# Seven block products added up in PSUM instead of on VectorE, and the low part of x by an accumulating transfer

## Chip, cores and metric

One core of one Trainium2 chip. The metric is the device time of one execution in microseconds (us). The engines are TensorE (PE; PEld are its weight loads), VectorE (DVE), ScalarE (ACT), GpSimd (POOL) and SyncE (SP); the last three also issue transfers.

## The reference

A linear attention with a decaying state, whose output, one row per token, goes through a two-layer network with a per-channel PReLU.

```
B, H, S, D = 4, 8, 768, 48
for t in range(S):
    state = sigmoid(f_logit[t])[:, None] * state + outer(k[t], v[t])
    y[t] = q[t] @ state
x = y.transpose(0, 2, 1, 3).reshape(B * S, H * D)      # 3072 x 384
h = x @ w_in                                            # 384 x 2048
g = max(h, 0) + alpha * min(h, 0)
out = g @ w_out                                         # 2048 x 384
```

All inputs and the output are fp32.

## The kernel before, in words

The work is cut into 12 steps, 0 to 11. A step is one chunk of 128 tokens of one pair of batches (U = 2 rows of 128 tokens, so T = 256 tokens). Each step has an attention part and a network part. The network part of a step runs mostly beside the attention part of the next one.

**The order** of everything is written out by hand. `ORDER_WORDS` is a list of words; each calls one part of a step, or the next piece of a part that has several. The number ahead is the step. Each engine and each DMA queue takes its instructions in the order in which the words issue them; between engines there are only semaphores. Words that the text names: `r`, `u`, `d`, `o` and `y` are TensorE parts of the attention (raw scores, quad scores, increments, off-diagonal blocks, output `py`); `f` starts a step on ScalarE with the sigmoid; `ef`, `eq`, `ek`, `ev` are the loads of a step (issued by GpSimd from step 1 on); `X` sends the attention's output through DRAM into the token layout `xT` (in step 11 straight from `y`). Words with an `N` belong to the network:

- `Nx` (line 947, ScalarE): `xh`, the high part of x with the sign turned. `NY` (`low_of_x`, line 950): the low part, x + xh, written over `xT`. `NZ` (line 954, VectorE): the mix `xs` of both. These three exist from step 3 on.
- `Na0` to `Na7`: the first layer, eight pieces of 256 channels. From step 3 on each has two halves of six matmuls: the high weights with `xh`, then the low weights with `xT`. `Nq` scales the bank, `Nb` adds the third pass, with `xs`. Steps 0 to 2 use plain fp32.
- `Nr` (ScalarE) and `Nc` (VectorE): the PReLU, into `gate`.
- `Np`: the second layer. From step 1 on it is done by blocks: `gate` is four blocks a, A, b, B (half of the channels, row of tokens), w_out is cut into 2 x 2 blocks (b11 ... b22, with sums t1 to t4 made once), and seven products replace eight. `Nm`, `Nu`, `Nv`, `Nw` (line 1016, VectorE, in halves) are the sums of gate blocks. `product(to, of, by)` multiplies a gate block with a weight block, 16 matmuls, into the PSUM bank `to`.
- The sums of products into the output tile `o` (line 1030, VectorE; `Nk` and `Ng` at lines 1050 and 1054 are ScalarE copies), then `Ns1` and `Ns0`, the stores.

Products and pieces of the first layer share four PSUM banks (pool `psn`, `bufs=4`): a new one waits until the one four back is free.

Of the kernel before, what the change touches and what calls it, by code (L numbers as in the profile page):

```python
# [48 lines left out]
v3 2ek 1O 1O b5 0Nr7 0Nr6 0Nc6 0Nc6 b5 b5 0Np1 1H0 1H0 v4 2f 0Nc7 0Nc7 2f 1U1 1U1 0Np2 2F 2F b7 b7 2g 1U1 2F 2F 2F 1D
2F 1A0 2g 1A0 v5 2g 2g 2f 2h 2h 1H1 b6 1A0 1A1 0Np3 2p 1H1 2p 2q 0Np4 1D 2g b7 1H1 1H1 2f 1A1 2q 2G 1A1 1A1 2q b6 1y0  # L50
1y1 2G 0Np5 2G V v7 2G 1Y1 v6 0Np6 0Np7 1Y0 W1 W0 W2 2q W3 1M 1M 1M 2u0 2i 1X 1X 2i 2l 2l 2r0 2R0 2l 2l 2R0 1X 1X 1X
1X 2R0 1X 1X 1X 1X 1Na0 2R0 Y7 2t 2t 2t 2U0 2t Y4 1Na1 W7 2U0 0No0 1Na2 2k 2k 2u1 2U0 2U0 2l 2r1 3ef 2U0 2l 2k Z7 2U0
W6 Y6 3ek Y2 2U0 1Nr0 1Nc0 1Nc0 1Nr1 1Nc1 2D 2A0 2A0 2K 2K 1Na3 1Nc1 Z7 2K 2K 1Nr2 1Nc2 2A0 2A0 2R1 2R1 1Na6 Z2 1Nc2
# [107 lines left out]
def kernel(  # L161
# [779 lines left out]
    def network(n_, bp, c, x):  # L941
# [7 lines left out]
        def low_of_x():  # L949
            nc.vector.tensor_tensor(x["T"], x["T"].bitcast(F32), late["xh"].bitcast(F32), ALU.add)  # L950
# [78 lines left out]
        def plus(to, of, by, scale=UP):  # L1029
            nc.vector.scalar_tensor_tensor(to, banks[of][:, 0:DH], scale, by, ALU.mult, ALU.add)  # L1030
# [121 lines left out]
```

## Time and profile before

| | |
|---|---|
| median of three runs | 587.82 us (587.04 to 588.15) |
| profiled execution | 587.32 us, span 585.5 us |
| mean granted TensorE clock | 0.985 |
| instructions | 19400 |
| DMA | 60.53 MB, mean 103 GB/s |

The span runs from the first to the last instruction of the profiled execution; what its time has more (1.8 us) lies around it. In the rows, L and a number is the line of the kernel; a group of instructions is named by what it writes and reads; "x" and a number is its count, and the arrow after an idle time points to what ended the waiting. "PEld" work overlaps "PE" work.

### The profile page before, as it was taken

How to read it: one execution, taken by the hardware profiler on the slowest of the kernel's cores; microseconds unless marked ns; L12 is line 12 of the kernel's file. 1: busy time of each engine (PE TensorE's matmuls, PEld its weight loads, DVE VectorE, ACT ScalarE, POOL GpSimd, SP SyncE). 2: the span in 40 equal slices, each digit the busy share in tenths (PEclk: the TensorE clock that was granted, in tenths of full speed). 3: DMA queues.
4: the chain of work that ended last, by engine and by line, in shares of the span. 5: the costliest groups of instructions: out<-in, count | busy, mean ns of one | idle time of the engine just before them, and what ended most of it. 6: DMA issues, size and time to landing. Idle time of an engine off the chain costs nothing. (4 is left out here: it accounts for less than half of the span.)

```text
span 585.5 us, 19400 instructions
## 1 busy us (share of the span) xinstructions
PE 564.7 (96%) x8416; PEld 521.2 (89%) x8416; DVE 513.4 (88%) x1077; ACT 320.1 (55%) x607; POOL 50.1 (9%) x89
## 2 busy tenths in 40 slices
PE   8799999999999999999999999998999899999997
PEld 6678867788888899899899899998999899999997
DVE  7689899989989999999999989998999989976452
ACT  5779985674280574474384583465374376363330
POOL 7210000200100000000010010020010000000000
PEclk9679999999999999999999999999999999999999
DMA  8959301730532252251161262172073251231000
GB/s 294 362 163 328 128 1 43 182 83 28 120 104 82 74 138 82 76 135 57 47 191 57 66 158 55 53 192 77 28 175 90 78 130 32 68 74 30 28 1 27
DMA packets 66853, 60.53 MB, mean 103 GB/s; under 512 B 44400, under 2 KB 58352, under 8 KB 66768
## 3 DMA queue, kind: packets, MB, share of 16 engines
q1 hardware_dynamic: 59744, 37.16, 22.3%
q0 software_dynamic: 6288, 21.76, 12.6%
q8 instruction: 66, 1.08, 0.8%
q10 hardware_dynamic: 736, 0.37, 0.2%
q14 instruction: 19, 0.16, 0.1%
HBM read 44.99 MB, written 13.50 MB: 100 GB/s over the span
## 5 line engine op out<-in xcount | busy, mean ns | idle before, releaser
L990 DVE SCALAR_TENSOR_TENSOR gate<-gate,om,ph 128x256 f32<-128x256 f32 x192 | 83.7, 477 | 18.6 <-ACT gate L983 18.1
L983 ACT ACTIVATE gate<-ph 128x512 f32<-128x512 f32 x96 | 55.8, 598 | 33.3 <-PE ph L959 28.8
L973 ACT ACTIVATE ph<-ph 128x512 f32<-128x512 f32 x72 | 40.7, 580 | 49.6 <-PE ph L959 45.7
L959 PE MATMUL ph<-xh,hi 128*128 128x256 f32 x432 | 62.8, 286 | 3.2 <-DVE o L1030 1.3
L1016 DVE TENSOR_TENSOR gate<-gate 128x512 f32<-128x512 f32 x88 | 58.8, 685 | 7.1 <-PE pc L1022 4.0
L959 PE MATMUL ph<-xT,w_in_sb 128*128 128x256 f32 x288 | 64.5, 382 | 0.3 <-DVE gate L990 0.3
L1022 PE MATMUL pa<-w_out_sb,gate 128*128 128x192 f32 x352 | 61.5, 328 | 0.0
L959 PEld LDWEIGHTS ph<-xT,w_in_sb 128*128 128x128 f32 x288 | 53.9, 190 | 8.3 <-issue 0.4
L959 PEld LDWEIGHTS ph<-xh,hi 128*128 128x128 f32 x432 | 55.0, 189 | 5.9 <-issue 2.9
L959 PE MATMUL ph<-xT,lo 128*128 128x256 f32 x432 | 60.0, 280 | 0.0
L526 ACT COPY A<-q 48x512 f32<-48x512 f32 x44 | 27.2, 618 | 59.2 <-DVE q L496 58.8
L1022 PEld LDWEIGHTS pa<-w_out_sb,gate 128*128 128x128 f32 x352 | 57.2, 190 | 0.5
L959 PE MATMUL ph<-xs,sum 128*128 128x256 f32 x432 | 55.1, 278 | 1.5 <-DVE xs L954 1.5
L959 PEld LDWEIGHTS ph<-xT,lo 128*128 128x128 f32 x432 | 54.7, 188 | 0.3
L959 PEld LDWEIGHTS ph<-xs,sum 128*128 128x128 f32 x432 | 51.8, 188 | 2.1 <-ACT ph L973 1.4
L563 DVE COPY_PREDICATED scores<-inq,qu 128x224 f32<-128x224 int32 (+6 forms) x140 | 42.0, 300 | 2.8 <-PE qu L553 0.4
L544 DVE TENSOR_TENSOR scores<-scores,q 128x768 f32<-128x768 f32 (+5 forms) x60 | 37.2, 620 | 0.5
L718 DVE COPY_PREDICATED scores<-mraw,raw 128x256 f32<-128x256 int32 (+1 forms) x80 | 35.6, 445 | 1.5 <-ACT A L730 0.3
L730 ACT COPY A<-scores 32x256 f32<-32x256 f32 x80 | 32.2, 402 | 5.8 <-DVE scores L563 4.6
L410 DVE TENSOR_TENSOR qd<-qd,scores 128x768 f32<-128x768 f32 (+2 forms) x36 | 27.1, 753 | 6.0 <-ACT qd L398 6.0
L1022 PE MATMUL pe<-w_out_sb,gate 128*128 128x192 f32 x176 | 30.8, 328 | 1.0 <-DVE gate L1016 0.9
L1022 PE MATMUL pb<-t,gate 128*128 128x192 f32 x176 | 31.3, 331 | 0.0
(151 smaller groups left out, 1018.7 us busy)
## 6 DMA issues: line engine op xcount, KB each, us to landing
w_out_raw<-in_w_out SPq DMA_DIRECT2D x8, 767.8 KB, 8.7
w_in_raw<-in_w_in SPq DMA_DIRECT2D x8, 767.2 KB, 9.5
scores<-in_fT POOLq DMA_DIRECT2D x11, 512.0 KB, 4.9
q<-in_qT POOLq DMA_DIRECT2D x11, 512.0 KB, 6.2
k<-in_kT POOLq DMA_DIRECT2D x11, 512.0 KB, 7.5
turned<-q SPq DMA_DIRECT2D x40, 128.0 KB, 3.5
ksn<-turned SPq DMA_DIRECT2D x10, 512.0 KB, 3.6
out<-o SPq DMA_DIRECT2D x24, 192.0 KB, 2.0
```

The source lines that it names most:

```text
L410: nc.vector.tensor_tensor(qdv[d], qdv[d - 1][:, :, :, 1:5 - d], f[:, :, 1:5 - d].rearrange("p (g i) r -> p g i r", i=NB), ALU.mult)
L526: nc.scalar.copy(A[halves(cc)[1], :, par * HP:(par + 1) * HP, CH * cc:CH * (cc + 1)], x["q3"][rows(par)].rearrange("p (u h c) s t -> p u h ...
L544: nc.vector.tensor_tensor(to, of, spread(fq[:, :, 1:1 + n], n), ALU.mult)
L563: nc.vector.copy_predicated(ad[:, :, m:NB], inq[:, 0:n].bitcast(I32).unsqueeze(1).unsqueeze(3) .broadcast_to((128, H, n, 4)), of.rearrange ...
L718: nc.vector.copy_predicated(ad[:, :, :, d:4], diag[:, :, 0:n].bitcast(I32).unsqueeze(1).broadcast_to((128, H, NB, n)), rv[:, :, QO[d]:QO[d ...
L730: nc.scalar.copy(A[s_, u, :, s_].rearrange("p h (i t) -> p h i t", t=4), ad[s_])
L959: nc.tensor.matmul(banks[f][:, j * T:(j + 1) * T], lhsT=of[:, kt, 128 * j:128 * (j + 1)], rhs=by[:, kt], start=first_ and kt + j == 0, sto ...
L973: nc.scalar.activation(banks[f], banks[f], AF.Copy, scale=EPS - 1.0)
L983: nc.scalar.activation(to, of, AF.Relu, scale=-1.0)
L990: nc.vector.scalar_tensor_tensor(to[:, j], to[:, j], om[:, m:m + 1], of[:, j], ALU.mult, ALU.add)
L1016: nc.vector.tensor_tensor(block(to)[:, p], block(x_)[:, p], block(y_)[:, p], op)
L1022: nc.tensor.matmul(banks[to][:, 0:DH], lhsT=block(of)[:, f], rhs=of_w_out(by)[:, f], start=start and f == 0, stop=f == NH - 1, skip_group_ ...
```

## The change

Three things change.

The sums of products. Some products now add onto a bank that already holds another product (`start` is False), with a copy taken out in between where a partial sum is needed by itself. Product 1 goes to bank pc, is copied (`Nd`), product 2 is added onto it and copied again (`Ne`); product 0 goes to pa, is copied (`Nk`), product 4 is added and read (`Nh`), product 5 is added and read (`Ni`, `Nj`). Four VectorE sums (`g`, `h`, `i`, `L`) and four ScalarE copies (`d`, `k`, `e`, `j`) a step take the place of eight sums and two copies. `Nf` and `Nl` no longer exist. The signs of the sums m and u and of t4 turn so that the products can be added.

The low part of x. `NY` is now a transfer that GpSimd issues, which adds `xh` from SBUF onto `xT` in SBUF; it was a VectorE instruction.

The order. From the attention of step 1 on, the words stand in another order.

```diff
-        to, x_, y_, op = (("t3", b22, b12, ALU.subtract), ("t2", "t3", b11, ALU.add), ("t4", "t2", b21, ALU.subtract),
+        to, x_, y_, op = (("t3", b22, b12, ALU.subtract), ("t2", "t3", b11, ALU.add), ("t4", b21, "t2", ALU.subtract),
...
-            nc.vector.tensor_tensor(x["T"], x["T"].bitcast(F32), late["xh"].bitcast(F32), ALU.add)
+            nc.gpsimd.dma_start(out=x["T"].bitcast(F32), in_=late["xh"].bitcast(F32), accum_op=ALU.add)
...
-        def plus(to, of, by, scale=UP):
-            nc.vector.scalar_tensor_tensor(to, banks[of][:, 0:DH], scale, by, ALU.mult, ALU.add)
+        def copy(to, of):
+            nc.scalar.activation(to, banks[of][:, 0:DH], AF.Copy, scale=UP)
+
+        def plus(to, of):
+            nc.vector.scalar_tensor_tensor(to, banks[of][:, 0:DH], UP, to, ALU.mult, ALU.add)
...
-        for n, args in enumerate((("pa", "a", "b11"), ("pc", "A", "t3"), ("pb", "B", "t4"), ("pa", "b", "b21", False),
-                                  ("pd", "B", "t2"), ("pe", "a", "t1"), ("pf", "A", "b22"))):
+        for n, args in enumerate((("pa", "a", "b11"), ("pc", "A", "t3"), ("pc", "B", "t4", False), ("pb", "b", "b21"),
+                                  ("pa", "B", "t2", False), ("pa", "a", "t1", False), ("pd", "A", "b22"))):
...
-        for key, args in dict(m=("A", "A", "a", ALU.subtract), u=("B", "B", "A", ALU.add), v=("a", "a", "B", ALU.add),
+        for key, args in dict(m=("A", "a", "A", ALU.subtract), u=("B", "B", "A", ALU.subtract), v=("a", "a", "B", ALU.add),
...
-            k=lambda: nc.scalar.activation(side("01"), banks["pa"][:, 0:DH], AF.Copy, scale=UP),
-            d=lambda: plus(side("11"), "pc", side("01"), -UP),
-            e=lambda: plus(side("10"), "pb", side("11"), -UP),
-            f=lambda: plus(side("11"), "pe", side("11")),
-            g=lambda: nc.scalar.activation(side("00"), banks["pa"][:, 0:DH], AF.Copy, scale=UP),
-            h=lambda: plus(side("10"), "pd", side("10")),
-            i=lambda: plus(side("11"), "pd", side("11")),
-            j=lambda: plus(side("01"), "pd", side("01")),
-            l=lambda: plus(side("01"), "pe", side("01")),
-            L=lambda: plus(side("01"), "pf", side("01")),
+            d=lambda: copy(side("11"), "pc"),
+            k=lambda: copy(side("00"), "pa"),
+            e=lambda: copy(side("10"), "pc"),
+            g=lambda: plus(side("00"), "pb"),
+            h=lambda: plus(side("10"), "pa"),
+            i=lambda: plus(side("11"), "pa"),
+            j=lambda: copy(side("01"), "pa"),
+            L=lambda: plus(side("01"), "pd"),
```

The new order around the low part of x in step 6:

```
... 6y0 5Nk 6y1 7g 7g 7h 6Y0 6Y1 5Np3 5Nv1 5Np4 7g 7p 5Ne 5Nv0 7p 7q 7G 7q 5Nh 6M 7h 7r0 7R0 6X 6X 5Np5 7i
7q 7q 5Ni 7i 5Np6 6M 6X 6Nx 7R0 6Na0 6NY 6M 7R0 7l 7u0 7u1 7R0 5Nj 5NL 6Na7 5Ns1 6Na2 6Na1 7ev 6Na0 ...
```

More of the change, by code (lines that the diff above doesn't have):

```diff
@@ L49 @@
[L49 to L53, printed above, removed]
@@ new lines @@
+1R0 1R0 1m a4 0Na0 1p a3 1g 0Na1 b2 2ek 1p b7 a3 w3 1R1 0Nr2 1R0 w4 0Nc2 0Nc2 a5 a6 1R1 0Nr0 1p a5 b1 b1 0Nr1 1j 0Na4
+b5 a7 v0 1R1 0Nc1 a6 0Nc1 1l 0Nr4 2f 0Na3 1l a7 1k w6 0Na6 0Nc0 1q 0Nc0 1K1 1q w5 1K0 1p b3 b3 0Na5 1o w7 0Nr3 1R0 b2
+v1 b4 b2 0Nc3 0Nc3 1s 1u0 b4 0Nr6 b5 0Nc4 0Na7 1O 1s 1O 0Np0 1d v3 0Nc4 b7 b7 b6 1s 1U0 1U0 1U0 0Nc6 0Nc6 0Nr5 1O 1H0
+1H0 1H0 1s 1u1 0Nc5 v2 1O 1H0 v4 b6 v7 2F 2f 2f 2F 1D 2f 2F 2F b5 2F 0Nr7 1D 2f 1U1 2g 2F 2g 2g 2g 1U1 1U1 v5 1t 0Nc5
+1H1 1t 1A0 0Nc7 1H1 1A0 0Nc7 1A1 2h 2p 2p 2q V 2q 1H1 2q 2q 2h 1H1 0Np1 1A0 2G 0Np2 0Np3 1A1 2G 2G 1A1 0Np4 1A0 1y0
@@ new lines @@
+1A1 1y1 1M 0Np5 2r0 1M 1M 2g 2u0 b6 v6 2R0 2R0 2R0 1Y1 2R0 2G 2U0 2U0 1Y0 2U0 2U0 2i 2i 2U0 2l Y4 1X 1X 1X 0Np6 1X 1X
+1X 1X 2l 2l 2l 1X 1X 1X W0 1Na3 2U0 0Np7 2t 2t 2t 2u1 W2 2U0 2t 2l 2l 2r1 2A0 W4 3ef 2k 2k Y7 2A0 2A0 2A0 2R1 1Na0
+1Na1 1Na2 0No1 1Nr3 2k 2K W6 Y2 1Nc3 1Nc3 2K 1Nr0 1Na4 1Nr1 1Na5 1Nc0 2R1 1Na6 3f 1Nr2 Z7 Z2 1Nc0 1Nr5 2R1 2K 2K 3eq
+W1 2o 2R1 3ev 2K 2U1 1Nr4 1Nc1 2U1 2d 3f 2U1 3f 1Nc1 0No0 W7 3F 1Nc2 1Nc2 1Na7 2U1 Y5 W3 1Nr6 2U1 2O 2O 2D 2U1 2O 1Nm0
+Z7 3g 2U1 2A1 3ek 2A1 W5 1Nc5 1Nc5 1Nc4 2D 2D 3F 1Nc4 1Nm1 1Np1 2O Z2 2A1 3F 3F 2A1 3F 3F 3f 3f 1Nr7 1Nc7 1Nc7 3g 3g
@@ new lines @@
+1Nc6 3G 3g 3h 2y0 2y1 2Y0 1Nc6 Y0 1Np0 1Nd 3G 2Y1 3r0 3p 3g 1Nk 3p 3R0 3q 1Np3 3q 3q Y1 3h 3R0 3R0 Y6 Z6 Z5 Z1 3q 3R0
+2X 2X 2X 3G 3G 1Np2 1Nu0 3u0 Y3 1Nu1 1Ne 3i 1Nw0 3i 1Nw1 1Np4 Z3 3l 1Ng 3l 3t Z1 3U0 1Np6 3t 1Nv0 1Nv1 2Na5 3l 3l 3l
+3t 1Nh 3t 3k 1Np5 3U0 Z3 3U0 2Nr5 4ev 3k 2Na1 Z0 3U0 2M 1Ni 3l 3U0 3k 1Nj 3U0 3U0 3K 3K 2Nc5 3K 2Na2 2M 2Nc5 Z4 3ev 3K
+2M 3u1 3r1 2Na0 3A0 2Nr2 4ef 3A0 Z4 2Nc2 2Nc2 3A0 3A0 Z6 2Nr0 1NL 3R1 Z0 3R1 3D 3R1 2Nc0 2Nr1 3R1 2Nc0 2Na3 3K 4f Z5
+3U1 3U1 3U1 3U1 2Na4 2Nc1 2Nc1 3U1 3U1 2Nr4 2Nm0 2Nr3 2Nc3 2Nc3 4eq 4f 4f 2Nc4 4g 3U1 4F 2Na7 4F 3o 3O 3O 2Nm1 3d 4F
@@ new lines @@
+3O 3O 2Nr7 3D 3D 4g 4F 3A1 3A1 2Nc7 3A1 2Np1 3A1 4g 4F 3y0 3y1 3Y1 4F 1Ns0 2Na6 S7 2Nc4 S1 3M S5 4g 1Ns1 2Nd 2Nr6 2Nc6
+3Y0 4f 4ek 4h 3X 2Nc7 2Np0 2Nc6 4h 2Np2 2Nu0 4f 2Np3 2Ne 4G 4G 4p 4G 2Nu1 4p 2Nw0 2Nw1 2Nv1 3M 4G 2Nv0 4r0 4R0 4q 2Nk
+2Np4 2Np6 4R0 3X 3X 3Nx 3NY 4g 4i 2Nh 4i 4q 4R0 4l 4q 4R0 4q 3Na1 2Np5 2Nj 4l 2Ng 3Na1 4u0 4t 3Na2 2NL 4t 4t 3M 4t 4l
+4U0 4U0 2Ni 4U0 3Na7 3Na2 S2 3Na7 5ev 4U0 2Ns1 2Ns0 4l 4l 4k 4U0 4l 4U0 4k 3Nq7 3Na0 4U0 3Na0 3Nq2 4u1 4ev 4r1 5ef
+3Nq1 3NZ 3Nb7 3Nq0 4k 3Nb2 4A0 4A0 4K 3Nb1 3Nr7 S0 3Nc7 3Nc7 3Nb0 3Nr2 3Nc2 3Nc2 3Na3 4A0 3Na3 3Nr1 4A0 3Nq3 S4 S3
@@ new lines @@
+5k 5l 5l 5u0 5l 4Na5 5ev 4Na2 5k 4Na0 5K 4Nq5 4Na1 4Nq0 4NZ 4Nb5 4Nb0 5K 5U0 4Nq2 4Nb2 5U0 4Nq1 4Nr0 4Nr5 5U0 4Nb1 5u1
+4Nr2 5K 5K 5K 5U0 5U0 5U0 5U0 5A0 4Na3 6ef 4Nr1 4Na3 5A0 4Nc0 4Na6 4Na6 4Nc5 4Nc5 4Nc2 5A0 5A0 4Nc2 4Nq6 4Nc0 4Nc1
+4Nq3 4Na4 4Nc1 4Nm0 4Na4 5D 4Na7 4Nq4 4Nb3 4Nr3 4Na7 6f 5R1 5R1 5R1 5R1 5U1 5U1 4Nb6 4Nr6 4Nb4 4Nc3 5U1 4Nc3 6eq 5U1
+5U1 5U1 4Nr4 6f 6f 4Nq7 6F 4Np0 4Nc6 5d 4Nm1 6f 6f 5U1 5o 6F 5A1 6g 5O 5O 6F 4Nb7 4Nc6 6g 5D 4Nc4 4Nr7 6F 4Nc4 5D 5A1
+6F 5O 6F 4Np1 5O 5A1 4Nc7 5A1 6G 6g 6G 6G 5y0 6g 4Nd 5y1 6G 6h 5Y0 5Y1 6g 4Nc7 4Np2 4Ne 6p 6h 4Nu0 5X 5X 4Nk 6p 6r0
@@ new lines @@
+4Nu1 4Np3 4Np4 6q 6i 4Nw0 5X 5Nx 6i 4Nw1 4Np6 5M 4Nh 6l 6l 6l 5Na0 4Nv0 4Nv1 6l 6t 6R0 6R0 6t 6t 6t 4Np5 4Ng 6q 6k
+5Na2 4Ni 6k 5Na1 6l 6q 5NY 4Nj 5Na1 5Na2 4NL 6l 5Na7 5Na0 6q 5Na7 6R0 6R0 4Ns0 5Nq2 6k 5Nq7 5Nq1 5M 5M 6u0 4Ns1 5NZ
+6u1 5Nb1 6U0 5Nq0 6K 6K 6U0 6U0 6U0 6U0 6U0 5Nb7 5Nr1 5Nb0 5Nr7 5Nr0 5Nb2 6r1 6U0 5Nc1 5Nc1 6D 5Na3 6A0 6A0 5Na3 5Nc7
+5Na6 6A0 5Na6 5Nc0 5Nc0 5Nr2 6A0 5Nc7 6R1 7ef 7f 6R1 6K 5Nq3 5Na5 5Nc2 5Nq6 5Na5 5Nb6 5Nc2 5Nb3 5Nq5 6K 6K 6R1 7eq 6R1
+5Na4 6U1 6U1 6U1 6U1 5Na4 5Nr6 6U1 6U1 5Nr3 7F 6d 6U1 7f 6o 5Nm0 5Nq4 5Nb4 7f 7f 7f 5Nc3 5Nc3 5Nm1 7F 5Nr4 7F 5Np1 7g
@@ new lines @@
+5Nb5 5Nr5 5Nc6 5Nc4 7F 5Nc4 6D 6D 6O 6A1 5Nc5 5Nd 5Nc5 7F 5Np0 7F 6A1 6A1 6O 6O 5Nc6 7G 7G 5Np2 6A1 7ek 5Nu0 7G 5Nw0
+5Nu1 7g 5Nw1 6O 6y0 5Nk 6y1 7g 7g 7h 6Y0 6Y1 5Np3 5Nv1 5Np4 7g 7p 5Ne 5Nv0 7p 7q 7G 7q 5Nh 6M 7h 7r0 7R0 6X 6X 5Np5 7i
+7q 7q 5Ni 7i 5Np6 6M 6X 6Nx 7R0 6Na0 6NY 6M 7R0 7l 7u0 7u1 7R0 5Nj 5NL 6Na7 5Ns1 6Na2 6Na1 7ev 6Na0 5Ng 7l 7t 7t 7t
+6Na2 7U0 7U0 7U0 7U0 7U0 7U0 7U0 7t 7l 7l 6Nq0 7A0 7A0 6Na7 8ef 6Nq2 7A0 5Ns0 6NZ 6Nb0 6Na1 6Nr0 6Nq1 7r1 7l 6Nb2 7k
+6Nb1 6Nq7 7A0 6Nb7 7k 7l 6Na6 7k 6Nc0 6Nc0 6Na5 6Nr2 7R1 6Nr1 7K 7K 6Na6 7R1 6Nc2 6Nc2 6Nc1 6Nr7 6Nc7 6Nc7 6Na3 6Na3
@@ new lines @@
+7Nq0 7NZ 7Nb1 7Nb7 7Nr1 9ef 7Nb2 7Nb0 8k 7Nr2 7Nr7 7Nr0 8k 8U0 8U0 7Na6 7Nc1 7Nc1 8U0 7Na6 8U0 7Nc2 8U0 8U0 8U0 8r1
+8A0 7Nc7 7Nc7 9ek 8A0 8A0 8A0 7Nc0 7Nc0 7Nq6 7Na3 7Na3 7Nc2 8R1 8R1 8R1 8R1 8U1 8U1 7Nm0 7Na5 8K 8K 8K 7Nq3 7Na5 9f
+7Nq5 7Nb3 9ev 7Nr3 9f 7Na4 8U1 7Nc3 7Na4 8U1 7Nb5 7Nc3 7Nq4 7Nb6 7Nm1 7Nr6 8U1 8U1 7Nb4 8U1 7Nr5 7Nr4 8D 7Nc6 7Nc6
+7Np1 7Nc4 8K 8K 8d 9eq 7Nc4 8o 8A1 7Nd 9f 9F 8A1 8A1 8O 8O 7Nc5 8O 7Nc5 7Np2 8D 8D 9F 7Nu0 8A1 9F 8O 8y0 9F 9F 9g 7Nw0
+9f 9f 9G 8y1 7Ne 8Y1 9G 9G 7Nu1 9G 10M 8Y0 7Np0 9F 7Np3 9g 9g 8M 9g 8X 9g 9h 8X 8X 9p 8M 7Nk 9p 9q 9r0 7Nw1 8Nx 7Np4
@@ new lines @@
+9h 7Np6 7Nv0 9q 7Nh 9q 7Nv1 7Np5 7Nj 9i 9R0 9R0 7Ng 9q 9i 8M 9R0 9l 8Na1 7Ni 8Na0 9u0 9R0 7NL 9u1 9l 9l 9l 9l 9l 8Na7
+9U0 8Na2 9t 7Ns1 9t 9t 9t 9U0 7Ns0 9U0 9U0 8NY 8Na0 8Na7 8Nq0 8Na2 8Na1 9U0 10ef 9U0 8Nq7 8Nq2 8NZ 8Nb0 8Nq1 8Nb2 9U0
+9k 8Nb7 8Nr0 9k 9k 8Nc0 9A0 8Nc0 9A0 8Nr7 8Nb1 9D 8Nr1 8Na3 8Na3 9r1 9A0 9A0 8Nc1 8Nc7 8Nq3 8Na4 10f 8Nc7 9ev 8Nc1
+8Na4 9R1 8Na5 9o 8Nr2 9K 9K 10f 9K 9K 9R1 9R1 10eq 9R1 8Nc2 8Na5 10F 8Nq4 8Nc2 8Nq5 8Nb3 9O 9U1 9U1 9U1 9U1 9U1 9U1
+8Nr3 8Nb4 8Nb5 8Nc3 8Nr4 9U1 8Nc4 8Nr5 8Nc5 8Nc3 8Nc5 9A1 9A1 9A1 9A1 9O 8Np0 9O 8Na6 10f 8Nm0 10f 8Nm1 8Na6 10f 8Nc4
@@ new lines @@
+9Na5 10ev 9Na5 10A0 9Nc3 10A0 9Nc0 9Nc0 9Nr4 10A0 9Na7 9Nq5 10R1 10R1 10R1 9Na6 10R1 10U1 10U1 9Nm0 9Na7 11ef 9Nc4
+11ek 11f 11f 9Nq7 9Nc4 9Na6 9Nq6 9Nb5 9Nm1 9Nr5 10K 10U1 10U1 9Nb7 10U1 10U1 9Nb6 9Np1 10U1 9Nr7 9Nc7 10d 10o 11F 9Nc5
+11eq 11f 11g 9Nc5 9Nd 9Nc7 9Nr6 11F 10A1 10D 10D 11g 10O 10O 10O 10O 11F 11F 11F 9Np0 10A1 10A1 9Nc6 11f 9Nc6 11g 11F
+9Nk 11g 9Np2 11f 9Nu0 10A1 10y0 10y1 9Nw0 11r0 10Y1 11h 9Nv0 10Y0 9Nu1 11ev 11G 11G 11G 9Nw1 10X 11R0 10X 11G 10X 11p
+9Np3 11M 11g 9Ng 11p 9Nv1 9Np4 9Ne 11R0 11R0 9Nh 9Np6 11q 11h 11i 9Np5 11i 11q 11l 11q 10Nx 11R0 9Nj 10Na0 11q 10Na3
@@ new lines @@
+11l 9NL 10NY 11t 9Ni 11l 9Ns0 11u0 11U0 11U0 9Ns1 11r1 10Na1 11t 11t 11U0 11U0 11U0 11U0 10Na4 11U0 11t 10Na1 11A0
+10Na0 10NZ 10Na3 11A0 11k 11A0 11l 10Nq1 10Nq0 11k 11k 10Nq3 10Na4 10Nb0 10Nb3 10Nq4 10Nr0 11A0 10Nr3 10Nc0 10Nc0
+10Nb4 10Nb1 10Nc3 10Na2 10Na2 10Nr4 10Nc3 11K 11K 10Na7 10Nc4 10Na7 11u1 11o 11K 11R1 11R1 11R1 10Nr1 10Na6 10Nq2
+10Nb2 10Nr2 10Na6 10Nq6 11R1 10Nq7 11O 10Na5 10Nc1 10Na5 10Nc1 11U1 11K 11O 10Nb6 10Nc4 10Nq5 11D 11U1 11U1 11U1 11U1
+10Nb7 11U1 10Nc2 10Nc2 10Nb5 10Nm1 11O 11O 10Nr7 11U1 11A1 11A1 11A1 11K 11d 10Nc7 10Nr5 10Np0 10Nc7 11D 11D 10Nm0
@@ new lines @@
+10Nk 10Nc5 11A1 11y0 11y1 10Nr6 10Nc5 11Y1 11Y0 10Nc6 10Nc6 10Np1 11X 11X 11X 10Np3 10Ng 11X 11X 10Nd 11X 11X 11X
+10Np2 10Nu0 10Nu1 11X 11X 10Np4 10Nw0 10Nw1 10Nv0 11Nx 10Np6 10Nv1 11NY 10Ne 10Nh 10Np5 10Nj 10Ni 10Ns1 11Na2 11Na3
+11Na0 11Na1 11Na0 11Nq0 11Na1 11Nq1 11Na2 11Nq2 11Na3 11Nq3 10NL 10Ns0 11NZ 11Nb1 11Nr1 11Nb0 11Nr0 11Nc1 11Nb3 11Nr3
+11Nc1 11Nb2 11Nc3 11Nc3 11Nr2 11Nc2 11Nc0 11Nc2 11Nm1 11Na5 11Na5 11Na4 11Nq5 11Na4 11Na6 11Nq4 11Na6 11Nb5 11Nr5
+11Nc0 11Nm0 11Na7 11Nc5 11Na7 11Nb4 11Nq6 11Nb6 11Nc5 11Nq7 11Nb7 11Nr4 11Nr6 11Np1 11Nc6 11Nr7 11Nc7 11Np0 11Nd 11Nk
@@ L123 @@
+11Nc7 11Nc6 11Nc4 11Nc4 11Np2 11Nu0 11Nw0 11Nu1 11Np4 11Nv1 11Nw1 11Ne 11Nh 11Np3 11Nv0 11Np5 11Ni 11Ns1 11Np6 11Ng
+11Nj 11NL 11Ns0
 """
```

89 lines of the change are left out of this document (16 added, 73 removed).

## The prediction

> **What bounds the kernel now.** I read the page first: the busy time of each engine, then the span in 40 slices.
>
> ```profile
> PE 564.7 (96%) x8416; PEld 521.2 (89%) x8416; DVE 513.4 (88%) x1077; ACT 320.1 (55%) x607; POOL 50.1 (9%) x89
> ...
> PE   8799999999999999999999999998999899999997
> ...
> DVE  7689899989989999999999989998999989976452
> ```
>
> TensorE (PE) is busy nearly throughout, and VectorE (DVE) is at nine tenths until the last six slices. Two engines are close to full at once, so I asked for busy time in two stretches: the steady part from 100 us, and the end.
>
> ```profile
> 100.00:482.00 382.00, 370.47 (x5788) 349.72 (x5787) 360.53 (x772) 204.03 (x392) 30.39 (x45) 1.00 0.37 97
> 482.00:582.00 100.00, 100.00 (x1267) 98.01 (x1265) 67.42 (x145) 39.76 (x80) 1.03 (x2) 1.00 0.14 40
> ```
>
> Columns: stretch, length, then busy us of PE, PEld, DVE, ACT, POOL, the granted clock, the DMA engines' busy share, GB/s. From 482 us on TensorE never stops; no change to VectorE can shorten that part. From 100 to 482 us TensorE is idle 382.00 - 370.47 = 11.5 us, and VectorE only 382.00 - 360.53 = 21.5 us. The clock is 1.00 in both, so it plays no part. Who ends TensorE's 11.5 us, by the waits of PE in that stretch:
>
> ```profile
> PE qu L553 <- DVE scores L544: 2.0, 4, 0.8
> PE py L739 <- ACT A L691: 1.6, 1, 1.6
> PE ph L959 <- DVE xs L954: 1.5, 2, 1.3
> PE ph L959 <- DVE o L1030: 1.3, 3, 0.6
> PE ph L959 <- issue: 1.3, 1, 1.3
> PE inc L652 <- DMA q<-in_qT: 1.2, 1, 1.2
> PE pe L1022 <- DVE gate L1016: 0.9, 2, 0.5
> PE ph L959 <- DVE gate L990: 0.8, 2, 0.5
> PE inc L652 <- DVE scores L563: 0.3, 1, 0.3
> ...
> PE py L739 <- DVE vs L670: 0.2, 1, 0.2
> ```
>
> (Total us, times, longest.) VectorE ends 2.0 + 1.5 + 1.3 + 0.9 + 0.8 + 0.3 + 0.2 = 7.0 us of it. One of these, 1.3 us, is TensorE waiting for a PSUM bank that a block sum of line 1030 still reads. So TensorE bounds the kernel, and VectorE, as a full second engine, makes it wait some 7 us.
>
> **The change, part by part.** TensorE: the same seven products of 16 matmuls in each of 11 steps; adding in PSUM only drops the start flag. Nothing removed, nothing added.
>
> VectorE and ScalarE: the rows of the sums, of the low part of x, and of the two copies:
>
> ```profile
> L1030 DVE SCALAR_TENSOR_TENSOR o<-pd,o x33: 340/348/358, 142.9 to 580.3; 128x192 f32<-128x192 f32 x33
> L1030 DVE SCALAR_TENSOR_TENSOR o<-pe,o x22: 343/347/358, 144.5 to 580.7; 128x192 f32<-128x192 f32 x22
> L1050 ACT ACTIVATE o<-pa x11: 314/330/388, 127.4 to 566.5; 128x192 f32<-128x192 f32 x11
> ...
> L950 DVE TENSOR_TENSOR xT<-xT,xh 128x768 fp32r<-128x768 f32 x9 | 8.6, 950 | 0.2
> ```
>
> (In the first three, ns are min/median/max.) The old code has eight such sums a step (pd three, pe two, and one each of pc, pb, pf), the new one four: 11 x 4 x 0.348 = 15.3 us gone. With the nine xT instructions, 9 x 0.950 = 8.6 us, VectorE loses 23.9 us. What falls before 482 us is the share of steps 1 to 9: 9 x 4 x 0.348 + 7 x 0.950 = 19.2 us, that is 5% of its 360.5, and its idle time there goes from 21.5 to about 41 us. ScalarE gets two copies more a step, 22 x 0.330 = 7.3 us; it is idle 178 us of the 382, so I cost them at nothing. If that cover fails (a copy stuck behind xh, which waits for its tokens), products 2 or 4, which may not write a bank before its copy is out, come late. VectorE's sum h likewise stands between products 4 and 5.
>
> Those three waits are the new ones on TensorE; behind them stand all later matmuls. The durations to weigh them with:
>
> ```profile
> 460.95 1.79 PE qu L553 x123
> ...
> 472.83 0.85 PE raw L700 x60
> ...
> 492.64 2.02 PE py L739 x64
> ...
> 497.46 2.60 PE pe L1022 x16
> ...
> 547.18 16.68 PE ph L959 x144
> ```
>
> (From the chain that ended last: start, us.) A product is 2.60, one half of an a word (six matmuls) 16.68 x 6/144 = 0.70, a u word 0.90, an r word 0.85. Counted in the new order, 1.5 us or more of other matmuls lie between products 1 and 2 in every step, 2.6 or more between 0 and 4, and 0.9 to 5.2 between 4 and 5. A copy or sum needs 0.35; only step 5, with 0.9, is tight when VectorE is inside a 0.95 us instruction. I put 0.5 us for all of this, with 0 and 4 us (11 steps x 0.35) as ends.
>
> The accumulating transfer. No such operation is in the trace, so I bound it by its neighbours, and then ask how long it may take:
>
> ```profile
> scores<-in_fT POOLq DMA_DIRECT2D x11, 512.0 KB, 4.9
> ...
> k<-in_kT POOLq DMA_DIRECT2D x11, 512.0 KB, 7.5
> ...
> w_in_raw<-in_w_in SPq DMA_DIRECT2D x8, 767.2 KB, 9.5
> ...
> xT<-tokens SPq DMA_DIRECT2D x9, 384.0 KB, 3.2
> ...
> L368 POOL DMA_DIRECT2D k<-in_kT x11 | 8.0, 725 | 25.1 <-DVE xs L954 19.6 <-ACT gate L983 4.5 <-ACT k L443 0.9
> ```
>
> It moves 384 KB and must also read its destination. Low end: 0.73 to issue + 3.2 (same size, plain) = 3.9 us. High end: the same bytes twice, 767 KB in a burst, 0.73 + 9.5 = 10.2. I take 0.73 + 4.9 = 5.6, the alone-standing load of 512 KB on the same queue, between once and twice the bytes. The Trainium skill ("DMA: Bandwidth & Descriptors", the anatomy of a GpSimd-issued DMA) gives about 2.0 us plus bytes over 436 GB/s, which is 2.9 us here; the sum would be the same, and the rows of this queue are slower than it (3.2 us by it for the 512 KB that took 4.9 and 7.5).
>
> How much may it take? The wait that counts is product lo x xT, the second half of the first a word. In the old trace:
>
> ```profile
> 172.09 2.08 PE L739 MATMUL py<-A,vs 128*64 128x64 f32 x64
> ...
> 182.56 0.84 ACT L947 ACTIVATE xh<-xT 128x768 fp32r<-128x768 f32 x1 [6.70 <-DMA xT<-tokens]
> ...
> 492.58 2.09 PE L739 MATMUL py<-A,vs 128*64 128x64 f32 x64
> ...
> 502.11 0.84 ACT L947 ACTIVATE xh<-xT 128x768 fp32r<-128x768 f32 x1 [4.08 <-DMA xT<-tokens]
> ```
>
> From the end of the py matmuls to the end of xh this takes 183.40 - 174.17 = 9.2 us at the longest of nine steps and 502.95 - 494.67 = 8.3 at the shortest of the usual ones. The new order puts, in step 6, between the last y word and the second half of 6Na0: products 5Np3 to 5Np6, 7r0, 7u0, 7u1 and four a halves = 10.4 + 0.85 + 1.8 + 2.8 = 15.9 us of matmuls. The same count gives 15.9 to 16.0 in steps 4, 5, 6, 7, 9 and 10, and 18.4 to 19.8 in 3, 8 and 11. So the transfer has 15.9 - 8.8 = 7.1 us on average (6.7 at worst) before TensorE waits. At 5.6 us it is hidden. If the cover is gone it costs (t - 7.1) us in each of six steps. Z, the mix, reads xT next on VectorE, with all of VectorE's queue behind it; TensorE needs its result 18.0 us or more after y, 18.0 - 8.8 - 0.95 = 8.2, so it is not first.
>
> On POOL's queue the transfer waits for xh with loads behind it (5ev, 4ev, 6ev, 7ef, 7ev, 9ef, 10ef, 9ev, 11ev, 10ev and what follows). Their first readers stand 8.6 us of matmuls (10f) to over 60 us behind it in the new order, against about 5 us of landing; nothing is late by that. Loads ahead of it are issued before the tokens arrive. SP's queue is not touched, but its stores share the DMA engines, busy 0.37.
>
> PSUM: six banks a step become four, so the 1.3 us wait for o goes. Of the other 5.7 us that VectorE ends I take two thirds, since its idle time doubles: 3.8. Sum: 1.3 + 3.8 - 0.5 = 4.6 us gained. The profiled execution took 587.32 (span 585.5), so 582.7; the median of three is 587.82, 0.5 above, so I forecast **583.0**. The ends of this term alone: nothing, if the freed time falls where TensorE already has work, and 11.5 us, if every idle time before 482 us goes.
>
> **The rivals.** *Dense TensorE.* The new order closes all 11.5 us: 587.8 - 11.5 = 576. For it: 41 us of slack on VectorE. Against it: 1.6 and 1.2 us wait for ScalarE and a load, 1.3 for issue. Chance 0.11.
>
> *No change.* VectorE's waits are placed by the order, a few tenths at a time, and it frees time where nobody waits: 587 to 589. Against it: line 1030 itself ends a wait of TensorE. Chance 0.12.
>
> *The transfer lands late* (slower). Point of decision: 6 x (t - 7.1) = 4.6, t = 7.9, a landing of 7.1 us. At the 7.5 of k it is 6 x 1.1 = 6.6, so 587.8 - 4.6 + 6.6 = 590; at t = 10.2 it is 6 x 3.1 + 1 = 20, so 603. For it: the destination is read too, and other loads run then. Against: 384 KB took 3.2. A rule of the Trainium skill ("SBUF — State Buffer", summary of rules) would make it longer: descriptors of a GpSimd DMA starve while VectorE is in a two-port mode, so use the other queues. Here the 32 KB pieces of xT issued by POOL and by SP and ACT can be compared:
>
> ```profile
> xT<-y ACTq DMA_DIRECT2D x6, 48.0 KB, 2.6
> xT<-y POOLq DMA_DIRECT2D x4, 32.0 KB, 2.3
> ```
>
> With one VectorE instruction of delay, 0.95, the 5.6 becomes 6.6, still under 7.1; the rows show no starving. Chance 0.14.
>
> *The new order is worse by itself.* From the last y word to the first a word it leaves 11.3 us in five steps, where the old one leaves 12.2 to 18.3; tokens and xh need 9.2 at worst. A step in which they take 1 us more than 11.3 costs that 1 us; 589 to 592. Chance 0.08.
>
> **How the numbers follow.** The forecast case (579 to 586) has 0.55; with the dense one, faster 0.66. A measurement of this kernel tells about 0.2% (1.2 us) from no change: within it 0.12, slower 0.22. Range 577 to 590: it leaves out half of the dense case and most of the late transfer.
>
> **What would show it.** Right: VectorE's busy time near 490 us, ScalarE's near 327, PE idle from 100 us on near 7 us, no wait of ph for o; the transfer landing in 4 to 6 us, and no PE wait for it. Wrong: waits of ph at line 959 for the transfer, of 1 us or more in six steps; waits of L1022 for o copies; or VectorE idle risen by 20 us while PE's idle stays at 11.

## The result, and the profile after

The changed kernel takes 578.99 us (median of four runs, 576.84 to 579.98), the kernel before 587.43 beside it: a ratio of 0.9856 [0.9819, 0.9894], 8.4 us less. The forecast was 583.0, a gain of 4.6. The direction held, and so did the main mechanism; the size was nearly twice the forecast. The profiled execution took 579.5 us.

The page of the changed kernel, its span, busy times and slices:

```profile
span 577.7 us, 19389 instructions
...
PE 564.1 (98%) x8416; PEld 521.7 (90%) x8416; DVE 497.0 (86%) x1024; ACT 324.6 (56%) x629; POOL 58.8 (10%) x98
...
PE   8799999999999999999999999999999999999997
...
DVE  6689899999979999999999979999999899884243
```

The span is 7.8 us shorter. VectorE (DVE) has 53 instructions fewer, ScalarE 22 more, GpSimd (POOL) nine more. The two later eights of TensorE's row in before are nines now. The steady part, first with the bounds used for before, then with bounds 8 us earlier, and the end (columns as before):

```profile
100.00:482.00 382.00, 378.35 (x5900) 358.83 (x5897) 358.74 (x746) 215.96 (x425) 36.96 (x52) 1.00 0.41 106
...
100.00:474.00 374.00, 370.35 (x5734) 351.22 (x5732) 351.63 (x730) 210.99 (x413) 36.96 (x52) 1.00 0.41 107
474.00:574.00 100.00, 100.00 (x1264) 97.90 (x1263) 61.88 (x132) 40.00 (x83) 2.93 (x4) 1.00 0.19 46
```

Up to 482 us TensorE is idle 382.00 - 378.35 = 3.7 us where it was 11.5, and the last 100 us, in which it never stops, start 8 us sooner. That is the whole gain. The two middle rows hold a lesson on VectorE: it is idle 374.00 - 351.63 = 22.4 us (6.0%), against 21.5 (5.6%) before. The time freed on VectorE did not turn into idle time; the same work of TensorE was over 8 us sooner. What TensorE still waits for between 100 and 482 us (total us, times, longest):

```profile
PE pa L1022 <- DVE gate L990: 1.4, 1, 1.4
PE ph L959 <- DVE xs L954: 0.8, 1, 0.8
PE pc L1022 <- DVE gate L990: 0.6, 1, 0.6
PE raw L700 <- DVE scores L563: 0.4, 1, 0.4
PE pa L1022 <- DVE o L1033: 0.3, 1, 0.3
PE qu L553 <- PE ph L959: 0.2, 1, 0.2
```

Of before's list only the wait for `xs` and a short one for `scores` are left. Line 1022 is the products, 1030 the copies, 1033 the four sums. No wait for the accumulating transfer (line 950) is in the list. Its instruction (ns, min/median/max; first and last start in us):

```profile
L950 POOL DMA_DIRECT2D xT<-xh x9: 924/929/951, 182.4 to 530.5; - x9
```

And its landing, with that of the plain load of the same tile (the last column is us):

```profile
xT<-tokens SPq DMA_DIRECT2D x9, 384.0 KB, 3.3
...
xT<-xh POOLq DMA_DIRECT2D x9, 384.0 KB, 4.1
```

0.93 us to issue and 4.1 to land make 5.0. The timeline shows the step with the least cover, step 4 (start, busy us; what it waited for in brackets):

```profile
230.78 2.87 PE L1022 MATMUL pa<-w_out_sb,gate 128*128 128x192 f32 x16 [0.30 <-DVE o L1033]
...
233.92 0.84 ACT L947 ACTIVATE xh<-xT 128x768 fp32r<-128x768 f32 x1
...
235.06 0.94 POOL L950 DMA_DIRECT2D xT<-xh  x1 [3.30 <-ACT xh L947]
...
240.06 3.01 PE L959 MATMUL ph<-xT,lo 128*128 128x256 f32 x24
```

From the end of `xh` (234.76) to the first matmul that reads the low part are 5.3 us; in the other eight steps the trace gives 7.0 to 11.7. Here the transfer just makes it, with TensorE at other work until then. (The first row is product 5 of step 3; the last experiment comes back to it.)

### The profile page after: what moved, and what is told of

It is laid out like the page before. It is cut to its first block, busy times and chain, and to the rows that moved or that the text cites. A ratio compares the mean times of both kernels' runs of the same rounds, so it can differ in the third digit from the quotient of the medians.

```text
span 577.7 us, 19389 instructions
## 1 busy us (share of the span) xinstructions
PE 564.1 (98%) x8416; PEld 521.7 (90%) x8416; DVE 497.0 (86%) x1024; ACT 324.6 (56%) x629; POOL 58.8 (10%) x98
## 4 chain that ended last, share of the span: by engine, by line
PE 57%; DVE 2%; DMA 1%; ACT 0%; issue 0%; DVEq 0%; ACTq 0%
PE ph L959 22%; PE pa L1022 11%; PE pc L1022 7%; PE pb L1022 4%; PE pd L1022 4%; PE py L739 2%; PE qu L553 2%; PE raw L700 2%; PE inc L652 1%; DMA out<-o 1%; PE off L682 1%; DVE o L1033 0%; DVE scores L544 0%; ACT gate L983 0%; DVE q L496 0%; DVE xs L954 0%
## 5 line engine op out<-in xcount | busy, mean ns | idle before, releaser
L1022 PE MATMUL pc<-t,gate 128*128 128x192 f32 x352 | 62.1, 329 | 0.6 <-DVE gate L990 0.6
L959 PE MATMUL ph<-xT,lo 128*128 128x256 f32 x432 | 58.6, 279 | 0.0
L1022 PEld LDWEIGHTS pc<-t,gate 128*128 128x128 f32 x352 | 57.0, 190 | 1.8 <-DVE gate L990 1.2
L959 PE MATMUL ph<-xs,sum 128*128 128x256 f32 x432 | 56.9, 281 | 0.8 <-DVE xs L954 0.8
L1030 ACT ACTIVATE o<-pa 128x192 f32<-128x192 f32 x22 | 7.3, 331 | 62.8 <-PE pa L1022 43.1
```

Source lines behind the costliest of these rows:

```text
L959: nc.tensor.matmul(banks[f][:, j * T:(j + 1) * T], lhsT=of[:, kt, 128 * j:128 * (j + 1)], rhs=by[:, kt], start=first_ and kt + j == 0, sto ...
L1022: nc.tensor.matmul(banks[to][:, 0:DH], lhsT=block(of)[:, f], rhs=of_w_out(by)[:, f], start=start and f == 0, stop=f == NH - 1, skip_group_ ...
```

## The experiments

Two theories of the 8 us. L: VectorE's lighter load brings them. O: the new order does. (The new order stands here for the order together with the products that add onto a bank; no run separates the two.) The first four kernels change one of the two at a time. Ratios are against the kernel before in the same session; it took 587.43 us beside the changed kernel, 586.88 beside the next eight and 585.84 beside the last ones. Differences between two other kernels are those of their medians, and so hold to some 2 us.

**The low part of x on VectorE again, all else as changed.**

```diff
-            nc.gpsimd.dma_start(out=x["T"].bitcast(F32), in_=late["xh"].bitcast(F32), accum_op=ALU.add)
+            nc.vector.tensor_tensor(x["T"], x["T"].bitcast(F32), late["xh"].bitcast(F32), ALU.add)
```

> The changed kernel with the low part of x on VectorE again, at the same place of the order (8.6 us of VectorE work back, no accumulating transfer). If VectorE's load is what matters (theory L), about a third of the gain goes: 581 to 583 us. If the new order brought the gain (theory O), 578 to 580. If the transfer itself delays TensorE somewhere, this is faster than 579: 576 to 578.

583.93 us, ratio 0.9958 [0.9935, 0.998]: 4.9 us above the changed kernel for 9 x 0.95 = 8.6 us of VectorE. Its steady part:

```profile
100.00:482.00 382.00, 375.42 (x5818) 354.95 (x5801) 359.73 (x746) 210.88 (x413) 29.63 (x44) 1.00 0.37 99
```

TensorE's idle time is 6.6 us in place of 3.7, though VectorE's busy time in these 382 us hardly differs from the changed kernel's 358.74: it is nearly full in both, and gets less far in one.

**Each of the four sums done twice** (the second adds the bank times 0.0).

```diff
             nc.vector.scalar_tensor_tensor(to, banks[of][:, 0:DH], UP, to, ALU.mult, ALU.add)
+            nc.vector.scalar_tensor_tensor(to, banks[of][:, 0:DH], 0.0, to, ALU.mult, ALU.add)
```

> The changed kernel with each of the four VectorE sums of a step followed by a second one of the same shape that adds zero times the bank (44 x 0.35 = 15.3 us of VectorE work back, as many sums as before the change). Theory L: two thirds of the gain go, 583 to 586 us. Theory O: 578 to 580.

588.5 us, ratio 1.0034 [1.0014, 1.0053]: 9.5 us above the changed kernel for 44 x 0.348 = 15.3 us of VectorE, and TensorE idle for 9.6.

```profile
100.00:482.00 382.00, 372.44 (x5701) 351.73 (x5684) 362.51 (x765) 210.26 (x412) 36.48 (x52) 1.00 0.41 105
```

**Both edits: before's load of VectorE in the new order.**

> The changed kernel with both: the low part of x on VectorE and the four sums doubled, so VectorE has the load of the kernel before (about 514 us busy) in the new order. Theory L: the whole gain goes, 585 to 589 us, with some 7 us of PE waits on DVE between 100 and 482 us. Theory O: 578 to 581.

594.09 us, ratio 1.0138 [1.0104, 1.0171].

```profile
100.00:482.00 382.00, 367.21 (x5624) 345.94 (x5625) 362.39 (x758) 205.21 (x405) 28.32 (x42) 1.00 0.35 94
```

With the load of before, the new order is 7.2 us slower than the old one, and TensorE is idle for 14.8 us. In the new order 23.9 us of VectorE are worth 15.1: 0.63 us for one, as in the two runs before (0.57 and 0.62). A doubled sum also holds its bank for longer. By the lists of waits TensorE stands 2.0 and 4.6 us in the last two kernels at products and first-layer pieces that wait for sums and copies of `o`, against 0.3 in the changed kernel; so part of these two prices, and of the 7.2 us, may be time of banks and not of VectorE's queue. No run separates them.

**The lighter load in the old order.** The kernel before with three of its sums and the low part of x left out and a fourth sum turned into a copy; no transfer takes the place of the low part.

```diff
-            nc.vector.tensor_tensor(x["T"], x["T"].bitcast(F32), late["xh"].bitcast(F32), ALU.add)
+            pass
...
-            e=lambda: plus(side("10"), "pb", side("11"), -UP),
+            e=lambda: nc.scalar.activation(side("10"), banks["pb"][:, 0:DH], AF.Copy, scale=UP),
...
-            h=lambda: plus(side("10"), "pd", side("10")),
+            h=lambda: None,
...
-            j=lambda: plus(side("01"), "pd", side("01")),
-            l=lambda: plus(side("01"), "pe", side("01")),
+            j=lambda: None,
+            l=lambda: None,
```

> The kernel before, in its old order, with VectorE relieved by as much as the change relieves it: the sums h, j and l and the low part of x are left out, and e is a ScalarE copy of its bank (so the output lacks these terms). Theory L: 579 to 582 us. Theory O: 586 to 588, with TensorE's idle time between 100 and 482 us still near 11 us.

578.3 us, ratio 0.9863 [0.9826, 0.99]: the whole gain without the new order. O falls. (Nothing in this kernel waits for the low part either, but before's list of waits has none for line 950.) TensorE's waits between 100 and 482 us in this kernel:

```profile
PE py L739 <- ACT A L691: 2.1, 1, 2.1
PE inc L652 <- DMA ksn<-turned: 1.1, 1, 1.1
PE ph L959 <- issue: 0.9, 1, 0.9
PE pe L1022 <- DVE gate L1016: 0.3, 1, 0.3
PE qu L553 <- issue: 0.2, 1, 0.2
```

Of the 7.0 us that VectorE ended before, 0.3 are left. Waits for ScalarE, a transfer (of another tile) and issue are there as before, some 4 us. The changed kernel has the reverse: those are gone, as they are in the three kernels above, which have the new order with more load, and 3.5 us of waits for VectorE remain. So the lighter load clears VectorE's waits, and the new order trades one set of waits for another of about the same sum. All four times lie beyond the ranges given for L, by 0.7 to 5 us, on the side of a larger effect.

**The accumulating transfer alone, in the old order** (the kernel before with the one line of the transfer).

> The kernel before with one part of the change alone: the low part of x by the accumulating transfer, old sums, old order. The transfer took 0.93 us to issue and 4.1 to land in the changed kernel. The old order leaves 13.6 to 19.7 us of matmuls from the last y word to the first use of the low part, less 8.8 us for tokens and xh: 4.8 us or more in every step, so it is just hidden. Theory L (VectorE's load, 0.57 us of span per us of VectorE work): 8.6 x 0.57 = 4.9 us less, 581 to 584 us. Rival (the transfer needs the new order's places, above all on GpSimd's queue, where loads stand ahead of it): 586 to 592.

587.29 us, ratio 1.0008 [0.9983, 1.0033]. By L it should have gained 3 to 6 us. The timeline of step 9 shows where they went:

```profile
450.49 0.84 ACT L947 ACTIVATE xh<-xT 128x768 fp32r<-128x768 f32 x1 [7.27 <-DMA xT<-tokens]
...
458.79 0.73 POOL L368 DMA_DIRECT2D scores<-in_fT  x1 [16.44 <-PE qu L553]
459.52 0.97 POOL L950 DMA_DIRECT2D xT<-xh  x1
...
466.55 3.72 PE L959 MATMUL ph<-xT,lo 128*128 128x256 f32 x17 [4.21 <-DMA xT<-xh]
466.58 0.96 DVE L954 SCALAR_TENSOR_TENSOR xs<-xh,xT 128x768 fp32r<-128x768 f32 x1 [6.60 <-DMA xT<-xh]
```

`xh` is ready at 451.33, but the transfer's word stands in the old order behind loads of later steps. One of them, `11ef`, waits 16.4 us on GpSimd's queue for the matmuls that still read its tile, and the transfer is issued 8.2 us late. TensorE waits 4.2 us for it and VectorE 6.6; behind the wait, from 466 to 470 us, the granted clock is only 0.59 and 0.55. That this place ate the gain was tested with **the same kernel and one word moved**: `9NY` right behind `9Nx`, ahead of `10ev`, `11ev` and `11ef`.

> n5 (old order, old sums, transfer alone) with one word moved: 9NY right behind 9Nx, so that on GpSimd's queue it stands ahead of the loads 10ev, 11ev and 11ef. In n5 that transfer was issued behind 11ef, which waited 16.4 us for TensorE, and TensorE then waited 4.2 us for the transfer. If that queue place ate the gain: 581 to 584 us. If the transfer costs elsewhere (memory traffic, the other steps): 586 to 588.

581.05 us, ratio 0.9938 [0.9906, 0.9971]. The gain is there, 4.8 us by the medians and 3.6 by the ratio, for 8.6 of VectorE. L holds, and the place on the queue was the cause.

**The transfer made twice in the changed kernel**, to test how much cover it has (the low part has `xh` in it once too often).

```diff
-            nc.gpsimd.dma_start(out=x["T"].bitcast(F32), in_=late["xh"].bitcast(F32), accum_op=ALU.add)
+            for _ in range(2):
+                nc.gpsimd.dma_start(out=x["T"].bitcast(F32), in_=late["xh"].bitcast(F32), accum_op=ALU.add)
```

> The changed kernel with the accumulating transfer made twice, one after the other (the low part then holds xh once too often). It then takes about 10 us from xh to landing. By the prediction's 7.1 us of cover, 6 steps x (10 - 7.1) = 17 us and 1 more in the other three: 595 to 599 us, with PE waits of line 959 for the transfer. If TensorE's queue has more cover than that count (rival), under 588.

601.01 us, ratio 1.0238 [1.0193, 1.0284]. The waits of TensorE, and below them of VectorE, over the whole span (the line numbers are one higher here):

```profile
PE ph L960 <- DMA xT<-xh: 14.4, 6, 4.5
...
DVE xs L955 <- DMA xT<-xh: 5.8, 2, 2.9
```

Six steps, as the prediction had counted (4 to 7, 9 and 10), and 22 us in all, 2 us above the range expected. The profiled execution is 19.2 us longer than that of the changed kernel: 14.4 are these waits, and TensorE's busy time grew by 5.3, from 564.1 to 569.4. Behind the longest wait, in step 4, the granted clock is 0.50 from 244 to 248 us, and the 24 matmuls that took 3.01 us in the changed kernel (240.06 in the timeline above) take 5.49:

```profile
243.94 5.49 PE L960 MATMUL ph<-xT,lo 128*128 128x256 f32 x24 [4.52 <-DMA xT<-xh]
```

The rival of the late transfer was real, and 5 us of landing kept it away.

**More of the same.** If VectorE's time is worth 0.6 us for one, another sum should go. The gate sum `v` (a = a + B) is an addition in place, so it can be an accumulating transfer too, two of 256 KB a step. In the first of two kernels both halves go that way in steps 1 to 9, in the second one half. The words of the halves that go by transfer stand right behind those of the sum `u`, and product 5, which reads the sum, was put behind product 6 in steps 3, 5 and 6.

```diff
-            nc.vector.tensor_tensor(block(to)[:, p], block(x_)[:, p], block(y_)[:, p], op)
+            if to == x_ and op == ALU.add and h in (0, 1) and n_ in (1, 2, 3, 4, 5, 6, 7, 8, 9):
+                nc.gpsimd.dma_start(out=block(to)[:, p], in_=block(y_)[:, p], accum_op=op)
+            else:
+                nc.vector.tensor_tensor(block(to)[:, p], block(x_)[:, p], block(y_)[:, p], op)
```

> The changed kernel with the gate sum v (a = a + B, two halves of 0.685 us on VectorE) as two accumulating transfers of 256 KB in steps 1 to 9, put right behind u in the order, and product 5 put behind product 6. VectorE loses 9 x 1.37 = 12.3 us: by theory L 12.3 x 0.57 = 7 us, 571 to 574 us, if the transfers hide behind the 7 to 10 us of matmuls between u and product 5. If 512-byte pieces make the transfer land after 10 us or more, TensorE waits in each of nine steps: 585 to 600.

> The same with only the second half of v as a transfer (256 KB a step) and the first on VectorE at its earlier place: VectorE loses 9 x 0.685 = 6.2 us, by theory L 3.5 us, 574 to 577 us if hidden; 580 to 590 if the transfer lands late.

586.37 us, ratio 1.0009 [0.9983, 1.0034], and 586.9, ratio 0.9993 [0.9968, 1.0018]: 7 to 8 us worse than the changed kernel, where L had promised a gain. Both times lie in the ranges for a transfer that lands late, but no wait for a gate transfer is among TensorE's. What is there, in the kernel with both halves (lines 973, 968, 567, 684 and 961 are 959, 954, 553, 670 and 947 of the changed kernel):

```profile
PE ph L973 <- DVE xs L968: 2.7, 1, 2.7
...
PE qu L567 <- DVE vs L684: 1.4, 1, 1.4
PE ph L973 <- ACT xh L961: 1.2, 1, 1.2
```

Two things differ from the changed kernel: the transfers (with their words), and the moved product. Each was then tried without the other.

**Transfers without the moved product**: `v` by transfer in steps 1, 2, 4, 7, 8 and 9, where no product has to move; beside it, and part of it, a kernel with **one pair of words swapped** (`2Nc4` ahead of `S7`), to take away the 1.4 us wait of `pa`.

> The changed kernel with v as two accumulating transfers in steps 1, 2, 4, 7, 8 and 9 only, where product 5 stands behind product 6 in the order already (no product is moved), and with the word 2Nc4 ahead of S7 as in n10. VectorE loses 6 x 1.37 = 8.2 us. If the loss of n7 and n8 came from moving product 5 (theory M), 8.2 x 0.57 = 4.7 us less than n10: 571 to 574 us. If it came from the transfers themselves or from what they hold up on GpSimd's queue (theory Q), 578 to 588.

> The changed kernel with two words swapped: the second half of 2Nc4 ahead of S7. In the changed kernel's trace VectorE stands 3.45 us at S7 (a sum over the first layer's weights that waits for the last plain product of step 2) with 2Nc4 behind it, and TensorE waits 1.44 us for a bank that 2Nc4 frees. If VectorE's queue held TensorE there, 1.4 to 2 us less: 576.5 to 578; if another wait comes right behind, 578 to 579.

579.78 us, ratio 0.9891 [0.9851, 0.9931], and 578.53, ratio 0.9891 [0.9859, 0.9922]. The swap took the wait of `pa` away, and product 1 waited right behind it:

```profile
PE pc L1039 <- DVE gate L1004: 1.7, 2, 1.3
```

The transfers neither cost nor gained anything that these intervals (up to some 2 us to either side) show, though VectorE is 6 us less busy than in the changed kernel:

```profile
100.00:482.00 382.00, 378.97 (x5870) 359.75 (x5860) 352.98 (x737) 216.31 (x426) 49.13 (x61) 1.00 0.46 113
```

TensorE's idle time is 3.0 us, against 4.0 in the kernel with the swap alone: little is left to win here from VectorE. The range of 571 to 574 us, for a loss that came from the moved product, was missed, since it reckoned with 0.57 us for each us of VectorE; so this run does not yet say what the move costs.

**The moved product without transfers**: the changed kernel, with product 5 behind product 6 in steps 3, 5 and 6.

(Parts of three lines of the order:)

```diff
-3Np5 3Np6
+3Np6 3Np5
-5Np5 7i 7q 7q 5Ni 7i 5Np6
+5Np6 7i 7q 7q 7i 5Np5 5Ni
-6Np5 6Nj 8ev 7Na0 6Np6
+6Np6 8ev 7Na0 6Np5 6Nj
```

> The changed kernel with product 5 issued behind product 6 in steps 3, 5 and 6, and nothing else; no block sum by transfer. It separates what the two kernels with v by transfer (586.4 and 586.9) had in common besides the transfers. If moving the product cost the 7 us there (theory P: product 5 and what reads its bank come later, VectorE gets its work in bunches), this kernel takes 584 to 587 us, with TensorE idle between 100 and 482 us up from about 4 to 8 or more. If the transfers did it (theory D: DMA issue on GpSimd or later sums in steps 3, 5 and 6), it takes 577 to 581 us, as the changed kernel does.

586.63 us, ratio 1.0009 [0.9984, 1.0034]: the move alone costs what the two kernels had lost. The timeline of step 3's network, beside step 4's attention, shows how:

```profile
233.32 2.76 PE L1022 MATMUL pa<-w_out_sb,gate 128*128 128x192 f32 x16
...
236.12 0.33 ACT L1030 ACTIVATE o<-pa 128x192 f32<-128x192 f32 x1 [10.49 <-PE pa L1022]
236.34 0.83 ACT L947 ACTIVATE xh<-xT 128x768 fp32r<-128x768 f32 x1
236.48 0.36 DVE L1033 SCALAR_TENSOR_TENSOR o<-pa,o 128x192 f32<-128x192 f32 x1 [1.67 <-ACT o L1030]
...
237.23 3.33 PE L959 MATMUL ph<-xh,hi 128*128 128x256 f32 x24 [1.15 <-ACT xh L947]
...
246.06 0.96 DVE L954 SCALAR_TENSOR_TENSOR xs<-xh,xT 128x768 fp32r<-128x768 f32 x1 [2.12 <-DMA out<-o]
...
247.16 2.96 PE L959 MATMUL ph<-xs,sum 128*128 128x256 f32 x24 [2.16 <-DVE xs L954]
```

Product 5 starts 2.5 us later than in the changed kernel (233.32 against 230.78 in the timeline shown above). Its copy `j` stands on ScalarE's queue ahead of `xh` (236.34 against 233.92), so `xh` is 2.4 us later, and TensorE waits 1.2 us for it at the first layer of the next step. The sum that reads the same bank holds VectorE for 1.7 us. The wait of 2.2 us is another one: `xs` and `o` share one buffer in the kernel, so `xs` waits until `o` of step 3 is stored, and with the late product the last sum of that `o` is 2.2 us later (VectorE waits 2.12 us for the store, against 1.02 in the changed kernel). The prediction had thought of a copy stuck behind `xh`; here `xh` is stuck behind a copy. In step 5 it is VectorE's queue that is held: the sum that waits for product 5 has `vs` behind it, and TensorE waits for `vs`:

```profile
326.52 0.36 DVE L1033 SCALAR_TENSOR_TENSOR o<-pa,o 128x192 f32<-128x192 f32 x1 [1.64 <-PE pa L1022]
326.91 0.55 DVE L670 TENSOR_TENSOR vs<-vs,inc 48x384 f32<-48x384 f32 x1
...
328.56 1.08 PE L553 MATMUL qu<-scores,k 48*32 48x112 f32 x64 [1.37 <-DVE vs L670]
```

A wait of 1.5 us for `A`, at 402 us, comes ahead of product 5 of step 6 (416 us), and what makes it stays open.

No kernel of these is faster than the changed one by more than the intervals allow.

## Why the prediction was right or wrong

**What bounds the kernel: right.** TensorE, with VectorE as a second full engine. The time follows TensorE's idle time before 482 us as load is put back on VectorE: 3.7 us at 579.0, 6.6 at 583.9, 9.6 at 588.5, 14.8 at 594.1.

**VectorE's waits: taken too small.** "Of the other 5.7 us that VectorE ends I take two thirds", 3.8: in the changed kernel all but the 1.2 us for `xs` and `scores` are gone, that is 4.5, and the lighter load in the old order left 0.3 of all 7.0. The 1.3 us for a bank that `o` holds went as forecast.

**Waits of others: left out, and the largest miss.** The forecast kept 1.6 for `A`, 1.3 for issue and 1.2 for a load. In the changed kernel all three are gone, 4.1 us for which the sum had nothing. The lighter load in the old order, where their like remain, and the heavier loads in the new order, where they are missing, put that down to the new order.

**New waits of the products: too low.** 0.5 was put for copies and sums. TensorE waits 0.3 us for a bank, but 1.4 + 0.6 for the gates of products 0 and 1, which the new order brought and the prediction did not look for. The wait for a bank came in step 3, and not in step 5, which it had called tight. By the lists of waits, then, 5.8 us of VectorE's and 4.1 of others went and 2.3 came: 7.6, where the sum had 5.1, nothing and 0.5. The errors partly cancel; that the forecast is only 4 us off is therefore in part luck. TensorE's idle time, forecast near 7 us, is 3.7.

**VectorE's load: right in instructions, wrong in the page's figure.** Counts times mean durations over all groups of VectorE fall from 581.6 to 557.5 us, by 24.1 (23.9 forecast). But the page's busy time counts overlapping instructions once, 513.4 before, and it fell by 16.4 to 497.0 and not to "near 490". The forecast took durations away from a union. ScalarE is at 324.6, near the 327.

**VectorE's idle time: wrong.** "From 21.5 to about 41 us" assumed that the steady part keeps its length. It got shorter instead.

**The transfer: right.** 0.93 + 4.1 = 5.0 us against 5.6; no wait of TensorE for it; six tight steps, seen when it was doubled. The 7.1 us of cover were too generous for one step, since step 4 had 5.3. The formula of the Trainium skill ("DMA: Bandwidth & Descriptors", the anatomy of a GpSimd-issued DMA) gave an estimate of 2.9 us; the trace has 4.1 and decides. The rule of the Trainium skill that the descriptors of a GpSimd DMA starve while VectorE is in a two-port mode ("SBUF — State Buffer", summary of rules) is not tested here. With VectorE busy for 94% of the steady part the nine transfers landed in 3.9 to 5.9 us, but no row tells in which mode VectorE's instructions ran. The two rows that the prediction compared for it are of 48 KB and 32 KB, not both of 32.

**The rivals.** Dense TensorE (576) came nearer than the forecast, 3 us against 4: of its 11.5 us, 7.9 went. The late transfer did not come about. No change is what the transfer alone gave in the old order, where loads stand ahead of it on GpSimd's queue; in the new order they were out of its way, as the prediction counted. The order that is worse by itself is true with the load of before, 7.2 us, and makes no difference that can be told (0.7 us) with the lighter one.

## What to carry to other kernels

When two engines are full together, read what the second one's instructions are worth from the first one's waits: here some 0.6 us for each us in the new order and 0.36 (8.6 for 23.9) in the old one, where the first 8.6 us gave 0.4 to 0.6 for each, and nothing that could be measured once the first engine has some 4 us of idle time left. The freed time then shows as a shorter span, and not as idle time on the engine that was relieved. An edit that moves work to a queue is worth what its place on that queue allows: a transfer behind a load that waits for its tile lost all of the 5 us expected of it, and one product issued later in three steps, with the copy, the sums and the store that hang on it, lost 7.
